# First-chunk blocks moved by VectorE as 32-bit words, last output tile stored as 320 and 128 columns, fewer TensorE waits

## Chip, cores, metric

One core of one Trainium2 chip. The metric is the device time of one execution in microseconds (us), lower is better. Unless a text says otherwise, a time inside the kernel is counted from the start of the profiled execution's span, which is 1.3 to 1.4 us shorter than the device time (92.9 us of span, 94.27 us of time in the same execution of the kernel before).

## The reference

```python
def reference(x, w1, b1, w2, b2):       # B, S, D, F = 1, 2048, 448, 1792, bfloat16
    h = jnp.einsum("bsd,df->bsf", x, w1) + b1
    h = jax.nn.gelu(h, approximate=True)
    return jnp.einsum("bsf,fd->bsd", h, w2) + b2
```

## The kernel before

It works through four chunks of 512 rows of x. Layer 1 makes `g` (gelu of 14 tiles of 128 hidden features), layer 2 makes output tiles of 128 rows by 448 columns; there are 16 of those. Every matmul of the two layers uses one half of the array (64 of the 128 contraction rows), and matmuls of the two halves run side by side, each into its own PSUM bank: in the trace a pair of 512-column ones starts every 216 ns, a pair of 448-column ones every 189. So "a pair" below is two half-array matmuls. The first chunk of x is turned by TensorE in 128x128 blocks into PSUM (the memory that matmuls write) and moved from there to SBUF (the working memory) by VectorE (DVE) and ScalarE (ACT); later chunks are turned by DMA.

A small recorder emits the waits. Each dependency of an operation becomes a wait of its own where its value is new, so an operation that needs two events of one semaphore can get two waits, and one of them becomes a standalone TensorE instruction (31 of these stand in the trace of before):

```python
for o in ops:
    for e in o.after:
        key, s, value = self.where[e.event if isinstance(e, Op) else e]
        if seen.get(key, 0) < value:
            eng.wait_ge(s, value)
            seen[key] = value
    ...
```

The moves of turned blocks (`e.copy` on ScalarE, `e.tensor_copy` on VectorE, bfloat16):

```python
for i in range(n):
    pr.op(engine, lambda e, i=i: (e.copy if engine == "scalar" else e.tensor_copy)(o[:, i], f[:, i]), ...)
...
for k, engine in enumerate(("vector", "scalar", "vector")):   # second half's blocks: "scalar"
    turn_block(0, k, k, 0)
    drain_blocks(engine, 0, (k,), k)
```

The end of the last chunk. `p` is a pair of tiles 448 columns wide; `q` and `r` are single tiles, each as two banks of 224 columns. `part("a")` and `part("b")` are the two halves of the contraction:

```python
q, r = Layer2(c, (2,)), Layer2(c, (3,), True)
p.part("a", every); q.part("a", every); p.part("b", every)
r.bias()                       # bias of the right 224 columns, by a matmul
r.part("a", every); q.part("b", every); r.part("b", every)
# r's drain: VectorE adds the bias to columns 0:224, ScalarE copies 224:448, then one store of 448 columns by SyncE
...
pr.barrier("sync", ["out"])    # the end waits for every store
```

## Time and profile before

| | before |
|---|---|
| time, median of the first 6 executions | 93.95 us (93.71 to 94.33) |
| TensorE busy (page) | 89.9 of 92.9 us |
| TensorE instructions (957 matmuls, 957 weight loads, 31 standalone waits, a drain) | 1946 |
| last matmul starts / last receipt of the last store | 90.45 / 92.89 us |

A receipt is the step of a semaphore that tells that a part of a DMA has arrived.

The chain of waits of the kernel before (start us, us, what): from 5.91 us on TensorE is the chain, without a break, to the last addition.

```profile
4.87 0.82 PE u L217 x6
5.70 0.21 PE u L350 x8
5.91 84.84 PE u L217 x915
90.76 0.38 DVE out_sb L332
```

The same kernel's groups of instructions with forms kept apart (count | busy us, mean ns | idle before). They give the cost of the moves and of the last eviction:

```profile
L363 DVE COPY xT<-u 128x256 bf16<-128x256 bf16 x3 | 0.8, 291 | 1.2 <-PE u L350 1.2
L332 DVE TENSOR_TENSOR out_sb<-u,b_bc 128x224 bf16<-128x224 f32 x1 | 0.4, 391 | 0.6 <-PE u L217 0.6
```

The timeline of its tail (start us, us, engine, line, operation, count). A row merges neighbouring instructions: the SPq row is the stores of q (issued 90.16) and r (issued 91.21).

```profile
89.20 1.51 PE L217 MATMUL u<-w_sb,g 64*128 64x224 bf16 x28
90.16 1.39 SPq L281 DMA_DIRECT2D out_dram<-out_sb  x2
90.75 0.39 DVE L332 TENSOR_TENSOR out_sb<-u,b_bc 128x224 bf16<-128x224 f32 x1 [0.61 <-PE u L217]
90.78 0.34 ACT L335 CAST out_sb<-u 128x224 bf16<-128x224 f32 x1 [9.24 <-PE u L217]
```

The DMA view of its last microseconds (88 to 94): a store takes 1.7 us from issue to landing.

```profile
q1 hardware_dynamic: 576, 0.46, 23.1%
issues: line engine op xcount, KB each, median us to landing
out_dram<-out_sb SPq DMA_DIRECT2D x3, 112.0 KB, 1.7
```

### The profile page before, as it was taken

Reading aid. Unit: us, or ns where it says so; the run is one execution under the profiler, and the core shown is the slowest. Engines: PE = TensorE matmul, PEld = TensorE weight load, DVE = VectorE, ACT = ScalarE, POOL = GpSimd, SP = SyncE. Lnnn points to the kernel's source line nnn. Section 1 sums busy time; section 2 is a strip of 40 time slices with the busy share of each in tenths; the row PEclk is TensorE's granted clock in tenths of the full one; section 3 lists DMA queues with packets and bytes.
Section 4 is the critical chain, followed back from the end, with each engine's and each line's share of the span. In section 5 each row is a group of like instructions: output and inputs, shape, how many; then the busy total and the mean of one; then the engine's idle time right before and its main releaser. Section 6 shows DMA issues by size and latency. Waiting matters only on the chain.

```text
span 92.9 us, 2111 instructions
## 1 busy us (share of the span) xinstructions
PE 89.9 (97%) x957; PEld 79.7 (86%) x957; DVE 13.5 (15%) x34; ACT 38.4 (41%) x64; POOL 1.7 (2%) x8
## 2 busy tenths in 40 slices
PE   6999999999999999999999999999999999999990
PEld 2488888999998888999998888999998888999990
DVE  0156001000432000000333000000233000000421
ACT  6063988700004787800003787900001878900001
POOL 6000000000000000000000000000000000000000
DMA  2999999768557000000022000000023000000022
GB/s 43 346 265 275 377 351 120 142 100 79 103 82 218 19 7 0 0 0 0 7 99 99 0 4 0 7 0 0 0 99 106 0 0 0 0 0 7 22 77 99
DMA packets 12745, 7.32 MB, mean 79 GB/s; under 512 B 6977, under 2 KB 12545, under 8 KB 12737
## 3 DMA queue, kind: packets, MB, share of 16 engines
q1 hardware_dynamic: 11904, 6.80, 31.0%
q10 hardware_dynamic: 800, 0.39, 1.4%
q8 instruction: 7, 0.11, 0.5%
q0 software_dynamic: 32, 0.00, 0.0%
q14 instruction: 2, 0.01, 0.0%
HBM read 3.79 MB, written 1.84 MB: 61 GB/s over the span
## 4 chain that ended last, share of the span: by engine, by line
PE 97%; DVE 0%; issue 0%
PE u L217 92%; PE u L192 4%; PE u L350 1%; DVE out_sb L332 0%
## 5 line engine op out<-in xcount | busy, mean ns | idle before, releaser
L275 ACT ACTIVATE g<-u,b_f 128x512 bf16<-128x512 f32 x56 | 34.9, 685 | 39.6 <-PE u L217 39.6
L217 PE MATMUL u<-w_sb,g 64*128 64x448 bf16 (+1 forms) x504 | 43.4, 328 | 0.0
L217 PE MATMUL u<-xT,w_sb 64*128 64x512 bf16 (+1 forms) x360 | 43.0, 366 | 0.0
L217 PEld LDWEIGHTS u<-w_sb,g 64*128 64x128 bf16 x504 | 41.4, 94 | 1.4
L217 PEld LDWEIGHTS u<-xT,w_sb 64*128 64x128 bf16 x360 | 31.3, 95 | 5.2 <-issue 0.2
L318 DVE TENSOR_TENSOR out_sb<-u,b_bc 128x448 bf16<-128x448 f32 x14 | 8.1, 619 | 60.3 <-PE u L217 60.3
L217 PE MATMUL u<-xT,w1r 64*128 64x512 bf16 x56 | 12.8, 376 | 0.0
L217 PEld LDWEIGHTS u<-xT,w1r 64*128 64x128 bf16 x56 | 5.1, 94 | 1.0
L335 ACT CAST out_sb<-u 128x224 bf16<-128x224 f32 x1 | 0.3, 345 | 9.2 <-PE u L217 9.2
L192 PE MATMUL u<-const-bfloat16-1.0 128*128 128x512 bf16 (+1 forms) x8 | 3.4, 599 | 0.8 <-PEq L471 0.8
L192 PEld LDWEIGHTS u<-const-bfloat16-1.0 128*128 128x128 bf16 x8 | 1.0, 136 | 2.4 <-issue 2.4
L363 ACT COPY xT<-u 128x256 bf16<-128x256 bf16 x3 | 1.0, 374 | 2.3 <-PE u L350 2.3
L175 ACT ACT_TABLE_LOAD x1 | 1.3, 1283 | 0.7 <-PEq L471 0.7
L350 PEld LDWEIGHTS u<-ident,xn 64*128 64x128 bf16 x24 | 0.9, 127 | 0.7 <-issue 0.6
L187 DVE COPY xT<-xT 64x512 bf16<-64x512 bf16 x3 | 0.9, 289 | 2.5 <-DMA xT<-in_x_dram 2.4
L434 DVE COPY b_z<-b_bc 1x448 bf16<-1x448 bf16 x1 | 0.3, 269 | 6.6 <-DMA b_bc<-in_b_dram 6.6
L390 ACT COPY xT<-u 64x256 bf16<-64x256 bf16 x2 | 0.7, 368 | 0.8 <-DVE xT L363 0.8
L350 PE MATMUL u<-ident,xn 64*128 64x64 bf16 x24 | 1.1, 238 | 0.0
L363 DVE COPY xT<-u 128x256 bf16<-128x256 bf16 x3 | 0.8, 291 | 1.2 <-PE u L350 1.2
L326 DVE TENSOR_TENSOR out_sb<-u,b_bc 128x448 bf16<-128x448 f32 x1 | 0.6, 624 | 1.7 <-PE u L217 1.7
L181 DVE STREAM_TRANSPOSE b1t<-b1n 32x32 bf16<-32x32 bf16 x4 | 0.8, 202 | 0.1
L368 DVE COPY xr<-xn 128x256 bf16<-128x256 bf16 x1 | 0.2, 226 | 3.1 <-DMA xn<-in_x_dram 3.1
(18 smaller groups left out, 4.9 us busy)
## 6 DMA issues: line engine op xcount, KB each, us to landing
out_dram<-out_sb SPq DMA_DIRECT2D x16, 112.0 KB, 1.7
w_sb<-in_w_dram SPq DMA_DIRECT2D x2, 784.0 KB, 9.0
w_sb<-in_w_dram SPq DMA_DIRECT2D x1, 576.0 KB, 6.2
xn<-in_x_dram SPq DMA_DIRECT2D x1, 448.0 KB, 3.2
w_sb<-in_w_dram ACTq DMA_DIRECT2D x2, 192.0 KB, 4.0
w_sb<-in_w_dram SPq DMA_DIRECT2D x1, 384.0 KB, 5.0
xT<-in_x_dram SPq DMA_TRANSPOSE x12, 4.2
w1r<-in_w_dram SPq DMA_DIRECT2D x1, 160.0 KB, 5.3
```

The costliest lines, as they stand in the source:

```text
L175: pr.op("scalar", lambda e: e.activation(junk[:, :], one, ACT.Gelu_apprx_tanh), event="table")
L181: pr.op("vector", lambda e, q=q: e.transpose(b1t[32 * q:32 * q + 32, :], b1n[:, 32 * q:32 * q + 32]), after=["b1n"], event=("b1t", q))
L187: pr.op("vector", lambda e: e.tensor_copy(xT[0:H, KT, s0:s1], xT[H:P, KT, s0:s1]), after=after, event=event)
L192: pr.op("tensor", lambda e: e.matmul(unit[0][:, 0, 0:cols], lhsT=ones_w, rhs=ones_m[:, 0:cols], start=True, stop=True))
L217: o = pr.op("tensor", lambda e: e.matmul(unit[u][:, lo, cols], lhsT=lhsT, rhs=rhs, start=start, stop=stop, skip_group_check=skip), after=a ...
L275: pr.op("scalar", lambda e, lo=lo, ft=ft: e.activation(g[:, ft, c * SC:(c + 1) * SC], unit[u][:, lo, :], ACT.Gelu_apprx_tanh, bias=b1_f[:, ...
L318: pr.op("vector", lambda e, lo=lo, j=j: e.tensor_tensor(out=out_sb[:, j, :], in0=unit[u][:, lo, 0:D], in1=b2_bc[:, :], op=ALU.add), after= ...
L326: pr.op("vector", lambda e: e.tensor_tensor(out=out_sb[:, j, :].rearrange("p (two h) -> p two h", two=2), in0=unit[u][:, :, 0:DH], in1=b2_ ...
L335: pr.op("scalar", lambda e: e.copy(out_sb[:, j, DH:D], unit[u][:, 1, 0:DH]), after=[y[1]], event=("o", j, 1))
L350: pr.op("tensor", lambda e, half=half, rows=rows: e.transpose(o(half), i(rows), ident[rows, rows]), after=["ident"] + after, event=event i ...
L363: pr.op(engine, lambda e, i=i: (e.copy if engine == "scalar" else e.tensor_copy)(o[:, i], f[:, i]), after=[wait or ("xt", h, ks[-1])], eve ...
L390: e.copy(o, i) if engine == "scalar" else e.tensor_copy(o, i),
```

## The change

Intent: (1) move more blocks by VectorE, as half as many 32-bit words, and spare ScalarE; (2) at most one wait per semaphore and operation on TensorE; (3) a shorter tail: let the last thing evicted and stored be small. The diff's core (cut: renamings, the column bookkeeping of `Layer2`, the second row of the bias constant, the same 32-bit move in `turn_rest`):

```diff
@@ emit
             for o in ops:
+                need = {}
                 for e in o.after:
                     key, s, value = self.where[e.event if isinstance(e, Op) else e]
-                    if seen.get(key, 0) < value:
-                        eng.wait_ge(s, value)
-                        seen[key] = value
+                    if value > max(seen.get(key, 0), need.get(key, (s, 0))[1]):
+                        need[key] = (s, value)
+                for key, (s, value) in need.items():
+                    eng.wait_ge(s, value)
+                    seen[key] = value
@@ moves of turned blocks
+                pr.op(engine, lambda e: e.tensor_single_scalar(out(U32), in_(U32), 0, ALU.bitwise_or),
+                      after=after, event=event)
-            for k, engine in enumerate(("vector", "scalar", "vector")):
+            for k in (0, 2, 1):
                 turn_block(0, k, k, 0)
-                drain_blocks(engine, 0, (k,), k)
+                drain_block(("vector", "vector", "scalar")[k], 0, k, k, 0, ("xt", 0, k))
-            drain_blocks("scalar", 1, (0, 1), 3)
+            for k in (0, 1):
+                drain_block("vector", 1, k, 3, k, ("xt", 1, 1))
@@ first chunk
-        L[1].b_main(0, HC)
-        L[1].b_main(HC, SC)
+        L[1].b_main()
@@ end of the last chunk (LAST = 160)
-                q, r = Layer2(c, (2,)), Layer2(c, (3,), True)
+                q = Layer2(c, (2,), 0, DH)
+                r, t = Layer2(c, (3,), 0, LAST), Layer2(c, (3,), 2 * LAST, DH - LAST)
                 p.part("a", every)
                 q.part("a", every)
                 p.part("b", every)
-                r.bias()
+                r.bias(1)
+                t.bias(0)
                 r.part("a", every)
                 q.part("b", every)
+                t.part("a", every)
                 r.part("b", every)
+                t.part("b", every)
@@ drain of r and t
+                    store(j, [("o", j, d0), ("o", j, d1)], d0, d2, "sync" if d2 < D else "scalar")
```

So tile 15 becomes `r`, two banks of 160 columns stored by SyncE's queue, and `t`, two banks of 64 columns stored by ScalarE's queue. TensorE gets 51 matmuls more (57 in the tail, 6 fewer in the first chunk; each with a weight load) and 20 standalone waits less.

More of the change, by code (lines that the diff above doesn't have):

```diff
@@ L9 @@
 FP32 = mybir.dt.float32
+U32 = mybir.dt.uint32
 class Op:
@@ L96, in bass_standalone__dense_activation_gelu__prompt_kernel @@
     NWARM = 7
+    LAST = 160
     with ExitStack() as es:
@@ L278, in act, with store, __init__, cols @@
                     busy[(u, lo)] = ("g", c, ft)
-        def store(j, after):
-            pr.dma("sync", lambda e: e.dma_start(o0v[:, j, :] if j < STC else out2[j * P:(j + 1) * P, :], out_sb[:, j, :]), "out", after=after)
+        def store(j, after, d0=0, d1=D, engine="sync"):
+            rows = o0v[:, j, d0:d1] if j < STC else out2[j * P:(j + 1) * P, d0:d1]
+            pr.dma(engine, lambda e: e.dma_start(rows, out_sb[:, j, d0:d1]), "out", after=after)
         class Layer2:
-            def __init__(self, c, tiles, last=False):
-                self.c, self.tiles, self.last, self.u = c, tiles, last, next_unit()
+            def __init__(self, c, tiles, d0=0, n=D):
+                self.c, self.tiles, self.d0, self.n, self.u = c, tiles, d0, n, next_unit()
                 self.split = len(tiles) == 1
-                self.n = DH if self.split else D
+                self.last = self.split and n < DH
                 self.fresh = [True, True]
-            def bias(self):
-                mm(self.u, 1, 1, slice(0, DH), ones_w[H:P, :], b2_z[H:P, DH:D], True, False, free(self.u) + ["b2z"])
+            def cols(self, lo):
+                d = self.d0 + lo * self.n if self.split else 0
+                return slice(d, d + self.n)
+            def bias(self, half):
+                rows = slice(half * H, (half + 1) * H)
+                mm(self.u, 1, half, slice(0, self.n), ones_w[rows, :], b2_z[rows, self.cols(1)], True, False,
+                   free(self.u) + ["b2z"])
                 self.fresh[1] = False
@@ L302, in part @@
                         rows = slice(half * H, (half + 1) * H)
-                        d0 = lo * DH if self.split else 0
                         fin = name == "b" and ft == NFT - 1
                         after = [("g", c, ft), ("w2", ft - ft % 7)] + (free(u) if self.fresh[lo] else [])
-                        mm(u, lo, half, slice(0, n), g[rows, ft, j * P:(j + 1) * P], w2_sb[rows, ft, d0:d0 + n],
-                           self.fresh[lo], fin, after, ("y", c, self.tiles[0], lo) if fin else None)
+                        mm(u, lo, half, slice(0, n), g[rows, ft, j * P:(j + 1) * P], w2_sb[rows, ft, self.cols(lo)],
+                           self.fresh[lo], fin, after, self.done(lo) if fin else None)
                         self.fresh[lo] = False
@@ L310, in part, with done @@
                     self.drain()
+            def done(self, lo):
+                return ("y", self.c, self.tiles[0], self.d0, lo)
             def drain(self):
-                c, u = self.c, self.u
-                y = [("y", c, self.tiles[0], lo) for lo in (0, 1)]
+                u, n = self.u, self.n
                 if not self.split:
                     for lo in (0, 1):
-                        j = c * STC + self.tiles[lo]
+                        j = self.c * STC + self.tiles[lo]
                         pr.op("vector", lambda e, lo=lo, j=j: e.tensor_tensor(
                             out=out_sb[:, j, :], in0=unit[u][:, lo, 0:D], in1=b2_bc[:, :], op=ALU.add),
-                            after=[y[lo], "b2"], event=("o", j))
+                            after=[self.done(lo), "b2"], event=("o", j))
                         busy[(u, lo)] = ("o", j)
@@ L323, in drain @@
                     return
-                j = c * STC + self.tiles[0]
+                j = self.c * STC + self.tiles[0]
+                d0, d1, d2 = self.d0, self.d0 + n, self.d0 + 2 * n
                 if not self.last:
                     pr.op("vector", lambda e: e.tensor_tensor(
-                        out=out_sb[:, j, :].rearrange("p (two h) -> p two h", two=2), in0=unit[u][:, :, 0:DH],
-                        in1=b2_bc[:, :].rearrange("p (two h) -> p two h", two=2), op=ALU.add),
-                        after=y, event=("o", j))
-                    store(j, [("o", j)])
+                        out=out_sb[:, j, d0:d2].rearrange("p (two h) -> p two h", two=2), in0=unit[u][:, :, 0:n],
+                        in1=b2_bc[:, d0:d2].rearrange("p (two h) -> p two h", two=2), op=ALU.add),
+                        after=[self.done(0), self.done(1)], event=("o", j, d0))
+                    store(j, [("o", j, d0)], d0, d2)
                 else:
                     pr.op("vector", lambda e: e.tensor_tensor(
-                        out=out_sb[:, j, 0:DH], in0=unit[u][:, 0, 0:DH], in1=b2_bc[:, 0:DH], op=ALU.add),
-                        after=[y[0]], event=("o", j, 0))
-                    pr.op("scalar", lambda e: e.copy(out_sb[:, j, DH:D], unit[u][:, 1, 0:DH]),
-                          after=[y[1]], event=("o", j, 1))
-                    store(j, [("o", j, 0), ("o", j, 1)])
+                        out=out_sb[:, j, d0:d1], in0=unit[u][:, 0, 0:n], in1=b2_bc[:, d0:d1], op=ALU.add),
+                        after=[self.done(0)], event=("o", j, d0))
+                    pr.op("scalar", lambda e: e.copy(out_sb[:, j, d1:d2], unit[u][:, 1, 0:n]),
+                          after=[self.done(1)], event=("o", j, d1))
+                    store(j, [("o", j, d0), ("o", j, d1)], d0, d2, "sync" if d2 < D else "scalar")
         HALVES = (slice(0, H), slice(H, P))
@@ L356, in turn_block, with move, drain_block @@
                      ("xt", h, k) if t else None, ["x"] + list(wait))
-        def drain_blocks(engine, h, ks, u, wait=None):
-            n = len(ks)
-            o = xT[:, ks[0]:ks[0] + n, h * HC:(h + 1) * HC].rearrange("p k (t b s) -> p k b t s", b=2, t=2)
-            f = unit[u][:, :, 0:n * H].bitcast(BF16).rearrange("p b (k t s) -> p k b t s", k=n, t=2)
-            for i in range(n):
-                pr.op(engine, lambda e, i=i: (e.copy if engine == "scalar" else e.tensor_copy)(o[:, i], f[:, i]),
-                      after=[wait or ("xt", h, ks[-1])], event=("xT0", h, ks[i]))
-            busy[(u, 0)] = ("xT0", h, ks[-1])
+        def move(engine, out, in_, after, event):
+            if engine == "scalar":
+                pr.op(engine, lambda e: e.copy(out(BF16), in_(BF16)), after=after, event=event)
+            else:
+                pr.op(engine, lambda e: e.tensor_single_scalar(out(U32), in_(U32), 0, ALU.bitwise_or),
+                      after=after, event=event)
+        def drain_block(engine, h, k, u, i, after):
+            move(engine,
+                 lambda t: xT[:, k, h * HC:(h + 1) * HC].bitcast(t).rearrange("p (t b s) -> p b t s", b=2, t=2),
+                 lambda t: unit[u][:, :, i * H:(i + 1) * H].bitcast(t).rearrange("p b (t s) -> p b t s", t=2),
+                 [after], ("xT0", h, k))
+            busy[(u, 0)] = ("xT0", h, k)
         def turn_first():
@@ L370, in turn_first @@
                 xn[:, :, D3:D].rearrange("p (q two) h -> p q two h", two=2)), after=["x"], event="xr_in")
-            for k, engine in enumerate(("vector", "scalar", "vector")):
+            for k in (0, 2, 1):
                 turn_block(0, k, k, 0)
-                drain_blocks(engine, 0, (k,), k)
-            turn_block(1, 0, 3, 0)
-            turn_block(1, 1, 3, 1)
-            drain_blocks("scalar", 1, (0, 1), 3)
+                drain_block(("vector", "vector", "scalar")[k], 0, k, k, 0, ("xt", 0, k))
+            for k in (0, 1):
+                turn_block(1, k, 3, k)
+            for k in (0, 1):
+                drain_block("vector", 1, k, 3, k, ("xt", 1, 1))
         def turn_rest():
@@ L383, in turn_rest @@
                 turn(lambda half, q=q: spot(2, 1)[:, half, q, :], lambda rows, q=q: xr[rows, q, :], ("xr", q), ["xr_in"])
-            drain_blocks("vector", 1, (2,), 2, ("xr", 1))
+            drain_block("vector", 1, 2, 2, 0, ("xr", 1))
             for src, engine in enumerate(("vector", "scalar")):
-                i = spot(2, 1, HALVES[src])
                 for dst in (src, 1 - src):
-                    o = xT[HALVES[dst], KT, 0:SC].rearrange("p (q two b s) -> p b q two s", q=2, two=2, b=2)[:, :, :, src, :]
-                    pr.op(engine, lambda e, o=o, i=i, engine=engine:
-                          e.copy(o, i) if engine == "scalar" else e.tensor_copy(o, i),
-                          after=[("xr", 1), ("xT0", 1, 2)], event=("xR0", dst, src))
+                    move(engine,
+                         lambda t, src=src, dst=dst: xT[HALVES[dst], KT, 0:SC].bitcast(t).rearrange(
+                             "p (q two b s) -> p b q two s", q=2, two=2, b=2)[:, :, :, src, :],
+                         lambda t, src=src: unit[2][HALVES[src], :, H:2 * H].bitcast(t).rearrange(
+                             "p b (q s) -> p b q s", q=2),
+                         [("xr", 1), ("xT0", 1, 2)], ("xR0", dst, src))
             busy[(2, 1)] = ("xR0", 1, 0)
@@ L432, in bass_standalone__dense_activation_gelu__prompt_kernel @@
             else:
-                pr.op("vector", lambda e: e.tensor_copy(b2_z[H:H + 1, :], b2_bc[H:H + 1, :]),
-                      after=["b2", "b2z0"], event="b2z")
+                for row in (0, H):
+                    pr.op("vector", lambda e, row=row: e.tensor_copy(b2_z[row:row + 1, :], b2_bc[row:row + 1, :]),
+                          after=["b2", "b2z0"], event="b2z" if row else None)
             if c + 1 < NSC:
```

## The prediction

> **What bounds it.** TensorE, nearly everywhere. The page: PE busy 89.9 of 92.9 us; the chain of waits: PE 97%, one unbroken stretch of 915 matmuls from 5.91 to 90.75 us, then a DVE addition. In the timeline a pair of half-array 64x512 matmuls starts every 216 ns, a 64x448 pair every 189, a 64x224 pair every 96: columns/2.4 plus about 2.5 ns. I see no hole in that pacing after 8.7 us. What is left is the front (x lands at 4.00 us; the last of 20 first transposes starts at 4.59, layer 1 at 4.87; until about 6.2 us a 64x256 pair takes 213 ns, half rate) and the tail (last matmul starts 90.45, DVE addition 90.75-91.14, store issued 91.21, landed 92.91: 2.46 us).
>
> **Part 1, 32-bit moves on VectorE.** A DVE COPY xT<-u of 256 bf16 takes 291 ns; the 448-column fp32 addition takes 619-624[...]. [...] Expected: 291 -> 285-295 ns, no gain. Moving two of three 372 ns copies off ScalarE helps nothing: second-half blocks were ready at 5.51 and first used at about 6.52. Layer 1 starts with block 0 at 4.87 as before; block 1, now from DVE at about 4.94 instead of ScalarE at 4.91, is at most 0.03 us later, behind a running matmul. Merging six 256-column pairs into three 512-column ones: -8 ns.
>
> **Part 2, fewer waits.** Standalone TensorE semaphore instructions fall from 31 to 11. Around those after 8.7 us the matmul starts keep their pace[...]. The two near 8.2 us cost some 30 ns but wait on different semaphores and stay. Gain 0 to 0.03 us.
>
> **Part 3, the tail.** PE work: before, 28 pairs at 96 ns = 2.69 us. After, 28 at 69 (160 columns) + 28 at X (64 columns) + 0.03 for the second bias matmul. X is the uncertain term. Streaming alone gives 29 ns. The half-rate transposes, same shape, start every 26.5 ns, 53 a pair: either 64/1.2 (so 29 at full rate) or a floor per matmul. [...] X = 29-33, PE +0.14 us; were it 53, +0.75.
> Last eviction: 64 columns instead of 224: DVE 391 -> about 225 ns, ScalarE 345 -> about 215, and the matmul itself drains 0.07 earlier: -0.23 us. Last store: 256-byte rows instead of 896; before, its packets ran 0.50 us of 1.70. I estimate 1.5-1.6: -0.13. The 320-column store goes out about 0.3 us ahead and should land first. Net about -0.22 us.
>
> **Sum.** 93.87 - 0.22 - 0.02 = 93.63 us. Range 93.2 to 94.1. Chances: faster by over 2% 0.01, within 2% 0.98, slower 0.01.
>
> **In the profile.** Right: DVE moves about 290 ns; layer 1 still starts near 4.87; 64-column pairs every 29-33 ns; last matmul about 0.1 us later; last landing about 2.2-2.25 us after the last matmul starts.
>
> **What would make it wrong.** X = 53: about 94.2. A small store that takes as long as the large: +0.13. A different moment of the step to full rate (now 6.2 us): each 1 us later costs about 0.5.

"columns/2.4 plus about 2.5 ns" is fitted to the three spacings named with it (216, 189 and 96 ns), and the 69 ns for 160 columns, the 29 ns for 64 and the 0.07 us by which the last matmul ends earlier are estimates from that fit. Half rate is 213 ns for a pair of 256 columns, against 110 later; scaled by these two, the 53 ns of the transposes would become about 27, and each us at half rate loses about 0.5. At 224 columns starts of the two halves lie 6 to 7 ns apart, so 26.5 ns is not the least distance of any two matmuls. VectorE's additions took 624 ns for 448 columns and 391 for 224; the line through them, 1.04 ns a column, gives 225 for 64. ScalarE's 215 is an estimate without such a ground; 213 was measured.

## More of the kernel before

One more line of its page, which I read past when I predicted. It is in the list of DMA queues (packets, MB, share of 16 engines): seven packets of 16 KB, in which instructions were fetched.

```profile
q8 instruction: 7, 0.11, 0.5%
```

The trace's DMA records, 16384 bytes each, start these fetches at 12.0, 21.5, 33.1, 45.7, 58.5, 71.8 and 83.7 us, each after 190 to 280 more TensorE instructions (245 on average).

## The result

| | before | after |
|---|---|---|
| median of 6 executions | 93.95 us (93.71 to 94.33) | 95.06 us (94.52 to 95.45) |
| ratio | | 1.0109, 95% interval 1.0070 to 1.0149 |

A ratio here is the mean time of one kernel's fast runs over the mean of the other's fast runs of the same rounds, so not quite the ratio of the medians. The change made the kernel about 1 us slower: within 2%, but outside the predicted range of 93.2 to 94.1 us and in the wrong direction.

The profile after, beside the lines of before. The chain of waits: TensorE's unbroken stretch is as long as before (84.83 against 84.84 us).

```profile
4.85 0.64 PE u L222 x6
5.49 0.12 PE u L364 x8
5.61 84.83 PE u L222 x956
90.46 0.21 ACT out_sb L349
```

The groups: a 32-bit move takes 290 ns where the bfloat16 copy took 291; the last evictions fell to 226 and 213 ns.

```profile
L377 DVE TENSOR_SCALAR xT<-u 128x128 uint32<-128x128 uint32 x5 | 1.2, 290 | 0.6 <-PE u L364 0.6
L346 DVE TENSOR_TENSOR out_sb<-u,b_bc 128x64 bf16<-128x64 f32 x1 | 0.2, 226 | 0.1
L349 ACT CAST out_sb<-u 128x64 bf16<-128x64 f32 x1 | 0.2, 213 | 0.1
```

The timeline of the tail. The SPq row is the stores of q (issued 89.32) and of r (90.42); the ACTq row is the store of t, issued at 90.76. The last matmul starts at 90.22.

```profile
89.22 1.19 PE L222 MATMUL u<-w_sb,g 64*128 64x160 bf16 x45
89.32 1.44 SPq L287 DMA_DIRECT2D out_dram<-out_sb  x2
89.98 0.67 DVE L346 TENSOR_TENSOR out_sb<-u,b_bc 128x160 bf16<-128x160 f32 x2 [0.69 <-PE u L222]
90.04 0.63 ACT L349 CAST out_sb<-u 128x160 bf16<-128x160 f32 x2 [8.91 <-PE u L222]
90.76 0.37 ACTq L287 DMA_DIRECT2D out_dram<-out_sb  x1
```

Up to here everything is early: the last store of before was issued 0.76 us after its last matmul started, that of after 0.54 us. The time is lost behind it. The DMA view of 88 to 94 us:

```profile
q1 hardware_dynamic: 464, 0.33, 17.4%
q10 hardware_dynamic: 144, 0.03, 2.5%
q8 instruction: 1, 0.02, 1.5%
issues: line engine op xcount, KB each, median us to landing
out_dram<-out_sb SPq DMA_DIRECT2D x1, 112.0 KB, 2.5
out_dram<-out_sb SPq DMA_DIRECT2D x1, 80.0 KB, 1.7
out_dram<-out_sb ACTq DMA_DIRECT2D x1, 32.0 KB, 2.4
```

The smallest store, 32 KB, is listed with 2.4 us. (All stores count on one semaphore, and the view gives each store the next 16 receipts in order of issue, so a late receipt of any of them is charged to the last.) And a queue is there that was not there before: q8, one packet. The page after has eight instruction fetches instead of seven:

```profile
q8 instruction: 8, 0.13, 0.8%
```

The trace's records of single packets and semaphore receipts, which the views only sum up, show the rest. A store gives 16 receipts; I read them as one from each of 16 DMA engines, which carry 8 of its 128 rows each:

```
instruction fetch, 16384 bytes:     89.97 to 91.39 us
q's 896-byte rows:                  15 receipts 90.81-90.98; 120 rows by 90.61, eight more only 91.38-92.02, six of them about 0.1 us each (0.04 elsewhere)
receipts counted on from there:     30 between 91.84 and 92.27, then 92.64, 92.97, 93.17
last packet of any store:           92.41 us
```

All three of the last stores (48 receipts) are complete on fifteen engines by 92.27 us. The three receipts that are missing come up to 0.9 us later, one after another. The eight late rows of q start at 91.38 us, as the fetch ends at 91.39. The same picture stands in each of the six traces with a fetch among stores (after, e1, e2, e4, e5, e7): eight of a store's 128 rows are late, and the first of them starts 4 to 15 ns before the fetch's recorded end.

The count of instructions tells why the fetch is there. The changed kernel has 82 TensorE instructions more than before; its seventh fetch is at 84.15 us, close to that of before (83.7), and the eighth comes 290 instructions later, 30 instructions ahead of TensorE's end. The kernel before has 226 instructions left when its seventh fetch starts and ends without an eighth.

**Theory.** The additional matmuls of the split tile push TensorE's program over another block of instructions, and the fetch of that block holds one DMA engine during the last stores. The traces show packets of 16384 bytes on a queue of their own (q8), one for every 183 to 290 TensorE instructions, and TensorE's chain unbroken for 84.8 us while all of them start, seven before and eight after. Whether a fetch costs anything elsewhere is what the experiments test. **Rivals:** a store of 256-byte rows, or one on ScalarE's queue, is slow in itself; or the front is worse (the moves, the removed waits).

A second thing must be held apart: the step of TensorE from half to full rate, seen in the spacing of matmul pairs. In the profiled execution of before, 256-column pairs still start every 213 ns at 5.9 us and every 110 ns from 6.30 us; in that of after they start every 190 ns at 5.01 us and every 110 ns already at 5.20. In the nine profiles the step lies anywhere from before 4.1 us (e1, whose first transposes already run at full rate) to 6.7 us (e2), though e2 and after, which differ only in the queue of the last store, have the same front. What decides its moment is not shown. The first layer-2 matmul started at 16.28 us before and at 15.86 after. Over the nine profiles the first matmul on `w1r`, which ends the front, started at 7.70 to 8.48 us. That spread is as wide as the 0.7 us range of equal executions and may be most of it, which is not shown, since only one execution of each kernel was traced. An early step flattered the profiled execution of after, which at 94.52 us is the quickest of its six. So I compare tails (start of the last matmul to the last receipt), which it does not touch: **2.44 us before, 2.95 after.**

### The profile page after: what moved, and what is told of

It reads as the page before. It is cut to its first block, busy times and chain, and to the rows that moved or that the text cites. A ratio compares the mean times of both kernels' runs of the same rounds, so it can differ in the third digit from the quotient of the medians.

```text
span 93.2 us, 2195 instructions
## 1 busy us (share of the span) xinstructions
PE 89.6 (96%) x1008; PEld 76.4 (82%) x1008; DVE 14.3 (15%) x38; ACT 38.0 (41%) x63; POOL 1.7 (2%) x8
## 4 chain that ended last, share of the span: by engine, by line
PE 96%; ACT 0%; issue 0%
PE u L222 92%; PE u L197 4%; PE u L364 1%; ACT out_sb L349 0%
## 5 line engine op out<-in xcount | busy, mean ns | idle before, releaser
L222 PE MATMUL u<-w_sb,g 64*128 64x448 bf16 (+3 forms) x560 | 43.7, 312 | 0.0
L222 PEld LDWEIGHTS u<-w_sb,g 64*128 64x128 bf16 x560 | 37.8, 94 | 5.1
L222 PE MATMUL u<-xT,w1r 64*128 64x512 bf16 x56 | 13.6, 376 | 0.0
L349 ACT CAST out_sb<-u 128x160 bf16<-128x160 f32 (+1 forms) x2 | 0.5, 253 | 9.0 <-PE u L222 8.9
L375 ACT COPY xT<-u 64x256 bf16<-64x256 bf16 (+1 forms) x3 | 1.1, 370 | 3.5 <-PE u L364 2.3
L377 DVE TENSOR_SCALAR xT<-u 128x128 uint32<-128x128 uint32 (+1 forms) x7 | 1.8, 288 | 0.6 <-PE u L364 0.6
L346 DVE TENSOR_TENSOR out_sb<-u,b_bc 128x160 bf16<-128x160 f32 (+1 forms) x2 | 0.6, 275 | 0.8 <-PE u L222 0.7
```

Of the source, the lines that this page charges most:

```text
L222: o = pr.op("tensor", lambda e: e.matmul(unit[u][:, lo, cols], lhsT=lhsT, rhs=rhs, start=start, stop=stop, skip_group_check=skip), after=a ...
L346: pr.op("vector", lambda e: e.tensor_tensor(out=out_sb[:, j, d0:d1], in0=unit[u][:, 0, 0:n], in1=b2_bc[:, d0:d1], op=ALU.add), after=[self ...
L375: pr.op(engine, lambda e: e.copy(out(BF16), in_(BF16)), after=after, event=event)
L377: pr.op(engine, lambda e: e.tensor_single_scalar(out(U32), in_(U32), 0, ALU.bitwise_or), after=after, event=event)
```

## The experiments

All kernels gave the correct result. Each was timed in five rounds against the kernel before.

### e1: the fetch moved earlier

Waits on semaphore values reached long before were added, spread over the first half of the changed kernel's TensorE program. The lines write 390; in the trace 148 more waits stand as instructions of their own. They order nothing anew; they only count as instructions.

```diff
-            for o in ops:
+            for i, o in enumerate(ops):
+                if name == "tensor" and i >= 150 and (i - 150) % 3 == 0 and (i - 150) // 3 < 130:
+                    eng.wait_ge(self.sems["gpsimd"], 1)
+                    eng.wait_ge(self.sems["vector"], 1)
+                    eng.wait_ge(self.sems["scalar"], 1)
```

> The changed kernel with 148 more standalone TensorE waits, all long satisfied, in front of matmuls of the first half, so that the last 16 KB fetch of TensorE instructions (89.97 us in the changed kernel's trace, 30 instructions before TensorE's end) comes about 148 instructions earlier, near 88 us. Fetch theory (the fetch holds one of 16 DMA engines for 1.4 us, and the last three stores have a sixteenth of their rows queued behind it): last landing about 2.1 us after the last matmul starts instead of 2.96, time 0.7 to 0.9 us below the changed kernel, so a ratio to before of 0.996 to 1.002. Small-store theory (a store of 256-byte rows on ScalarE's queue is itself slow): unchanged, 1.008 to 1.013.

Measured: 93.91 us median, ratio 0.9998 (0.9967 to 1.0028). The fetch starts at 89.23 us, 1.57 us ahead of the last matmul, and takes 0.93 us. Tail 2.08 us. The same small store on the same queue, in the DMA view of 88 to 94 us, now lands in 1.5 us, with the fetch still in the window:

```profile
q10 hardware_dynamic: 144, 0.03, 2.5%
q8 instruction: 1, 0.02, 1.0%
issues: line engine op xcount, KB each, median us to landing
out_dram<-out_sb SPq DMA_DIRECT2D x2, 112.0 KB, 2.7
out_dram<-out_sb SPq DMA_DIRECT2D x1, 80.0 KB, 1.6
out_dram<-out_sb ACTq DMA_DIRECT2D x1, 32.0 KB, 1.5
```

The delay has gone to the earlier stores (2.7 us), where nothing waits for it. So 148 instructions that do nothing made the changed kernel about 1.0 us quicker (0.9998 against 1.0109); neither small stores nor ScalarE's queue are slow in themselves. This profiled execution also has an unrelated hole of 0.9 us at 10.2 us, where the last part of w1 landed late (11.06 us; 9.3 to 10.3 in the eight other profiles). Its table of waits (us in total, times, longest us):

```profile
PEld u L226 <- DMA w_sb<-in_w_dram: 1.4, 2, 1.0
```

### e2: the small store on SyncE's queue

```diff
-                    store(j, [("o", j, d0), ("o", j, d1)], d0, d2, "sync" if d2 < D else "scalar")
+                    store(j, [("o", j, d0), ("o", j, d1)], d0, d2, "sync")
```

> The changed kernel with the 128-column store issued by SyncE's queue. Fetch theory: still slow, ratio to before 1.006 to 1.013, the last receipts again from one engine some 0.7 us after the other fifteen. Queue theory (ScalarE's queue is the slow part): back to 0.997 to 1.001.

Measured: 94.99 us, ratio 1.0095 (1.0059 to 1.0132). The fetch starts 0.08 us ahead of the last matmul and takes 1.53 us; tail 3.08 us. Which of the two queues issues the small store makes no difference that the rounds show. One part of the expectation was too simple: here fifteen of the receipts of q come at 91.40-91.58 and only one late, but the 128-column store behind it in the same queue is late as a whole: its first packet leaves 1.71 us after issue, where a store otherwise needs 0.82 to 0.89. The trace shows where the time went: SyncE's issuing instruction took 1.21 us instead of 0.33 and ended 0.39 us after the fetch ended.

### e3: parts 1 and 2 alone

The changed kernel with the tail of before (`r` as two banks of 224 columns, one store, no `t`).

```diff
-                r, t = Layer2(c, (3,), 0, LAST), Layer2(c, (3,), 2 * LAST, DH - LAST)
+                r = Layer2(c, (3,), 0, DH)
+                r.last = True
-                t.bias(0)
...
```

> Parts 1 and 2 alone (32-bit moves, merged 256-column pairs, merged waits) with the old tail. My costing: 0.999 to 1.001 of before, no fetch after 84 us (1914 TensorE instructions, before has 1946). A theory that the front is to blame (DVE moves or a later step to full rate): 1.004 or more.

Measured: 93.96 us, ratio 0.9998 (0.9967 to 1.0030). The last fetch starts at 84.4 us, tail 2.45 us. The moves, the merged pairs and the merged waits are worth nothing that five rounds can show, in either direction. The front is not to blame.

### e4: the kernel before with the waits of e1

The same lines as in e1, in the kernel before (147 instructions more).

> Control: the kernel before with 147 more satisfied waits on TensorE. An eighth fetch should appear near 87 to 88 us, over before the last stores. Fetch theory with free waits: 0.999 to 1.002 of before. If the waits themselves cost, or any additional fetch costs wherever it falls: 1.004 or more.

Measured: 94.01 us, ratio 0.9995 (0.9967 to 1.0023). An eighth fetch appears at 87.28 us, takes 1.12 us and is over at 88.4, before the last two stores; tail 2.45 us. The 147 satisfied waits on TensorE and an additional fetch that falls before the tail cost nothing here that the rounds show.

### e5: part 3 alone

The changed kernel with the waits, the moves and the 256-column pairs of before: 20 waits and 6 matmuls more, so 2060 instructions.

```diff
-                need = {}                     # merged waits: taken back
...
-                pr.op(engine, lambda e: e.tensor_single_scalar(out(U32), in_(U32), 0, ALU.bitwise_or), ...)
+                pr.op(engine, lambda e: e.tensor_copy(out(BF16), in_(BF16)), ...)
-        L[1].b_main()
+        L[1].b_main(0, HC)
+        L[1].b_main(HC, SC)
```

> Part 3 alone (320+128 columns, two stores), with the waits, moves and 256-column pairs of before: 2060 TensorE instructions, 32 more than the changed kernel, all of the additional ones ahead of the tail, so the fetch begins 32 instructions earlier, 0.3 to 0.5 us before the last matmul instead of 0.25. Fetch theory: the tail (last matmul to last landing) is the end of the fetch plus about 1.7 us, so 2.4 to 2.7 us instead of 2.96; ratio to before 1.003 to 1.008, slower than before but less so than the whole change: the removed waits, harmless in themselves, made the whole change worse. If position did not matter: the same as the whole change, 1.009 to 1.013.

Measured: 94.23 us, ratio 1.0027 (0.9997 to 1.0057), just below the expected band, and not clear of no difference. It was run on another chip. The fetch starts 0.38 us ahead of the last matmul and took only 0.95 us; tail 2.41 us. This interval and that of the whole change (from 1.0070) do not overlap: taken alone, part 3 costs clearly less than with parts 1 and 2, which cost nothing by themselves (e3). The account that fits is that removing 32 harmless instructions moved the fetch towards the last stores, but it is not shown apart from chance: the fetch ended 0.57 us after the last matmul's start here and 1.17 us after it in the changed kernel, and of these 0.60 us only 0.13 are its earlier start; 0.47 are its length, which varies between executions.

### e6: no eighth fetch

Tile 14 as two half sums of 448 columns, one bank for each half of the contraction, added at the end: 28 matmuls fewer and one for the bias more, 1974 instructions. r, t and their two stores are those of the changed kernel.

```diff
-                q = Layer2(c, (2,), 0, DH)
+                qu, qs = next_unit(), sb("qs", [P, D], FP32)
+                def half_sums(fts):           # bank lo takes contraction half lo, all 448 columns
+                    ...
-                q.part("a", every)
+                mm(qu, 1, 1, slice(0, D), ones_w[H:P, :], b2_z[H:P, :], True, False, free(qu) + ["b2z"])
+                half_sums(every[:7])
...
-                q.part("b", every)
+                half_sums(every[7:])
+                pr.op("scalar", lambda e: e.copy(qs[:, :], unit[qu][:, 1, 0:D]), ...)
+                pr.op("vector", lambda e: e.tensor_tensor(out=out_sb[:, jq, :], in0=unit[qu][:, 0, 0:D], in1=qs[:, :], op=ALU.add), ...)
```

> The changed kernel with tile 14 computed as two half sums in two banks, 448 columns wide (28 matmuls fewer, 1974 TensorE instructions; ScalarE copies one bank, VectorE adds the other). Fetch theory: no fetch after 84 us, tail 2.05 to 2.15 us, last matmul as early as in the changed kernel at the same moment of the step to full rate; ratio to before 0.995 to 0.999, the best of all. If the two small stores are slow in themselves: 1.006 or more.

Measured: 93.83 us, ratio 0.9984 (0.9952 to 1.0016). The last fetch starts at 85.4 us, tail 2.06 us. The DMA view of 88 to 94 us has no q8, and the small store takes 1.5 us:

```profile
q1 hardware_dynamic: 576, 0.43, 21.7%
q10 hardware_dynamic: 144, 0.03, 2.5%
issues: line engine op xcount, KB each, median us to landing
out_dram<-out_sb SPq DMA_DIRECT2D x2, 112.0 KB, 1.7
out_dram<-out_sb SPq DMA_DIRECT2D x1, 80.0 KB, 1.6
out_dram<-out_sb ACTq DMA_DIRECT2D x1, 32.0 KB, 1.5
```

It is about 1.2 us quicker than the changed kernel. Against the kernel before it is the quickest of all in its mean, but its interval holds 1: a gain is not shown.

### e7: the fetch put back

e6 with 54 of the satisfied waits of e1 (limit 48 instead of 130), which makes 2028 TensorE instructions, as many as the changed kernel has.

```diff
+                if name == "tensor" and i >= 150 and (i - 150) % 3 == 0 and (i - 150) // 3 < 48:
...
```

> e6 with 54 satisfied waits put back on TensorE in the first half: 2028 TensorE instructions, exactly as many as the changed kernel; same matmuls and stores as e6. Fetch theory: the eighth fetch is back within 0.5 us of the last matmul, one engine's receipts come last by 0.4 to 0.9 us, tail 2.6 to 3.1 us instead of 2.06, ratio to before 1.004 to 1.010. If e6 was quick for another reason (fewer matmuls, fewer evictions): 0.996 to 1.000, as e6, and e4 shows that the waits themselves are free.

Measured: 94.84 us, ratio 1.0090 (1.0058 to 1.0123). It was run on another chip. The fetch is back, 0.01 us after the last matmul's start, and takes 0.97 us; tail 2.63 us. The DMA view of 88 to 94 us:

```profile
q8 instruction: 1, 0.02, 1.0%
issues: line engine op xcount, KB each, median us to landing
out_dram<-out_sb SPq DMA_DIRECT2D x2, 112.0 KB, 1.9
out_dram<-out_sb SPq DMA_DIRECT2D x1, 80.0 KB, 2.1
out_dram<-out_sb ACTq DMA_DIRECT2D x1, 32.0 KB, 2.1
```

Time and tail are as expected; how it happened is not quite. I expected one late engine. Here all sixteen receipts of the 320-column store come last (93.21 to 93.39), because its first packet leaves 1.62 us after issue, as the store behind a late one did in e2. Again the issuing instruction itself was held. The timelines of SyncE's queue show this store of e7, the 320-column store of e5, and for comparison the last store of the kernel before (start us, us):

```profile
91.00 1.12 SPq L291 DMA_DIRECT2D out_dram<-out_sb  x1
90.38 0.72 SPq L284 DMA_DIRECT2D out_dram<-out_sb  x1
91.21 0.33 SPq L281 DMA_DIRECT2D out_dram<-out_sb  x1
```

The fetches of e7 and e5 ended at 91.74 and 90.75 us, 0.38 and 0.34 us before these issues did; from the end of the issue to the first packet it took the usual 0.5 us. Still, with the matmuls and stores unchanged, 54 instructions that do nothing cost about 1 us (1.0090 against 0.9984); e4, with 147 of them and its fetch over before the last two stores, lost nothing that the rounds show.

### All together

Fetch start is counted from the start of the last matmul; "none" means that the last fetch is over 5 us earlier.

| kernel | TensorE instructions | fetch start, length (us) | tail (us) | ratio to before |
|---|---|---|---|---|
| before | 1946 | none | 2.44 | 1 |
| after | 2028 | -0.25, 1.42 | 2.95 | 1.0109 |
| e1 after + 148 waits | 2176 | -1.57, 0.93 | 2.08 | 0.9998 |
| e2 small store by SyncE | 2028 | -0.08, 1.53 | 3.08 | 1.0095 |
| e3 parts 1 and 2 | 1914 | none | 2.45 | 0.9998 |
| e4 before + 147 waits | 2093 | -2.92, 1.12 | 2.45 | 0.9995 |
| e5 part 3 | 2060 | -0.38, 0.95 | 2.41 | 1.0027 |
| e6 tile 14 as half sums | 1974 | none | 2.06 | 0.9984 |
| e7 e6 + 54 waits | 2028 | +0.01, 0.97 | 2.63 | 1.0090 |

With the split tile the tail is 2.06 to 2.08 us where the last fetch begins 1.57 us or more ahead of the last matmul, and 2.41 to 3.08 where it begins within 0.4 us of it.

## Why the prediction was wrong

Point by point:

- **The 32-bit moves: right.** 290 ns for 128 words against 291 for 256 bfloat16 values, so half as many elements took as long. Why is not shown. Layer 1 started at 4.85 us.
- **The waits: right in themselves, and incomplete.** They cost nothing that the rounds show (e3, with 20 fewer than before, 0.9998; e4, with 147 more, 0.9995). I did not see that each of them also counts towards the next fetch (148 of them moved it from 0.25 to 1.57 us ahead of the last matmul in e1), and that taking instructions away brings a fetch nearer to the end (30 instructions ahead of TensorE's end in the changed kernel, 49 in e5, which keeps them).
- **X, the time of a 64-column pair: right.** In the tail of after, starts of equal halves lie 29 ns apart (89.835, 89.864, 89.893), in the predicted 29 to 33 ns. The predicted +0.14 us on TensorE is nearly right: from the first layer-2 matmul, behind the step, to the last one it took 74.17 us before (as in e3 and e4) and 74.36 after, so 0.19 us is lost.
- **The evictions: right.** 226 and 213 ns against predicted 225 and 215. VectorE's started 0.29 us after the last matmul's start before and 0.21 us after, so 0.08 us earlier against the predicted 0.07.
- **The last store: wrong, and this is the step that failed.** I wrote "Last store: 256-byte rows instead of 896 [...] I estimate 1.5-1.6: -0.13" and that the 320-column store "should land first. Net about -0.22 us". From its issue to the last receipt of all it was 2.41 us in the changed kernel. The estimate of the store alone was good: 1.5 us in e1 and e6. What I left out is the fetch that the 82 additional TensorE instructions bring into this very stretch. It added 0.87 us to the tail in the trace (2.95 against 2.08) and turned the -0.22 us into a loss. (That the gain would have come without it is not shown by the rounds either: the intervals of e1 and e6 hold 1.) My list of what would make the prediction wrong had "+0.13" for a slow store; it had no other user of the DMA engines.

How far it is shown: e1 and e7 move or restore the fetch with instructions that do nothing, and the loss goes and comes with it. Some things stay open. The records do not name the DMA engine of a packet, so that the fetch and the late rows share one engine is inferred from the receipts (fifteen early, one late per store) and from the late rows, which start as the fetch ends. The delay takes a second form: in e2, e5 and e7 (and harmlessly in e4) SyncE's instruction that issues a store was held until 0.34 to 0.39 us after the fetch's end and took 0.72 to 1.23 us, and the first packet left 1.26 to 1.73 us after its start instead of 0.82 to 0.89, so that the whole store went late, while in the changed kernel the 320-column store was issued in the middle of the fetch in 0.33 us and only a sixteenth of it waited. What decides between the two I cannot say. In e1 rows that were due by 88.76 us left only at 90.14, though the fetch's record starts at 89.23, so the recorded length can be less than the time for which it holds others up. The sizes agree: from one trace of each kernel I get 0.19 us on TensorE and 0.51 us in the tail, 0.70 us together, at the low end of what the timed rounds say, 1.0 (0.66 to 1.4). The fetches took from 0.88 to 1.83 us in these profiles, so other executions may lose more; this was not traced.

## What to carry to other kernels

Count instructions when you split work into more of them: in this unrolled kernel the TensorE program came in by DMA, 16 KB for about every 245 instructions, and the page's line of the instruction queue, with the starts of its packets in the trace, tells where the next fetch falls. Ahead of the last two stores an additional fetch cost nothing that the rounds show (e4, 0.9995); among the last stores, which the end of the kernel waits for, it cost about 1 us (e7 1.0090 against e6 0.9984), more than the whole gain of 0.22 us hoped for from a shorter tail. When a DMA is slower than its size explains, list every queue in that stretch, look at which of its 16 receipts comes last, and at how long the instruction that issued it took.
